# Converting three weight sets of the second layer beside the seven-product phase, and spacing the third chunk's attention at four steps a slot

## The chip, the cores and the metric

The kernel runs on one core of one Trainium2 chip. Each core has five engines with a queue of their own that run in order: TensorE (PE, whose weight loads are shown apart as PEld), VectorE (DVE), ScalarE (ACT), GpSimd (POOL) and SyncE (SP, which here issues nearly all DMAs). The metric is device microseconds of one execution; lower is better.

## The reference, cut to what matters

```python
x = attention(q, k, v)                 # 4 batches, 8 heads, 576 positions, banded masks; (2304, 512)
h = x @ w_in;  g = h * sigmoid(h)      # first layer, 512 -> 2048
x = g @ w_out                          # 2048 -> 512
a = x @ w1;  b = x @ w2                # second layer, 512 -> 1024 each
out = (a * b @ w3) @ w_out2            # 1024 -> 1024 -> 512
```

The weights come in a wide format of two 32-bit words a number. All products are made from pairs of reduced-precision numbers: each operand is split into a high part and a low part (the rest), and a product takes three matmuls, high by high, high by low and low by high. Converting a weight therefore means: load 512 KB of raw words; one ACT operation that rebiases the high words in place (`rebias`); two DVE operations that put the bits together (`bits`); an ACT copy that rounds to the high part (`high`) and a DVE subtraction that leaves the low part (`low`).

## The kernel before

The order of all work is written out by hand; the engines follow it in order and wait on each other by semaphores.

**First layer.** The 2304 tokens go in five chunks `CH1` of 512, 512, 256, 512 and 512. A chunk runs over 16 blocks `f` of the inner dimension; a *slot* is one block: the first product of the next block (`h_part`, two halves `h` and `H`), tanh and a multiplication (`t`), the split (`g`) and the second product of this block (`x2_part`, halves `x` and `X`). The strings in `SLOT` say in which order a slot's pieces are emitted. The letter `a` emits the next step of the attention of later chunks. `ATT` lists the eight steps by which two units of attention go through: V and S (values, and the scores of the next pair), M (maximum), E and O twice (exponential, output of the pair before), N (normalise: two small DVE operations and one POOL product a unit), L (loads), T (transposes), W (evacuation). The next pair's V waits for this pair's W, and the scores of the pair after it are emitted with that V. The letter `p` emits one operation from a list `todo`: first sums of weights and later 22 operations `late` that make sums of activations, and after the last slot whatever is left of it and four operations `last_`.

The third chunk (c = 2) has 256 tokens, so its 24 matmuls a slot are shorter. Its slots (`SLOT[1]`) hold five `a` and four `p`. Going through the lists by hand: the attention steps end with slot 7 of its 15, and `late` is emitted four a slot in slots 7 to 12.

**Seven-product phase.** The fourth chunk's first product is made for blocks p and p + 8 together by seven products of half size (`HPROD`, `h_product`, loop over p = 0 to 7). The products S1 to S4 take sums of weights that `sums_ops` left in DRAM (`swd`); `load_sw` brings those of the next p into four tiles `sw0` to `sw3` of a pool `sp`. A product goes to one of four banks; `collect_h` takes it out with DVE and ACT, and the product four places later writes that bank. Between the products stand the matmuls of the fourth chunk's second product (`x_some`, 24 a p), on `ga` of the p before.

**Late stage.** Sixteen blocks of the fifth chunk's second product, 12 matmuls each, and beside each block up to seven operations (`LATE_MICROS`) of the `Jobs` object `cv2`, which converts the second layer's weights: eight pieces of the output weights (WO), the sixteen pieces of w3, and eight *sets* a to h. A set holds a block of w1 or w2 for seven products: it is made from two raw pieces, with sums (`combine`), 7 units of 512 columns in all, and is also stored to DRAM (`setd`, by `set_io`) since it is used in three rounds. Its target is a pair of tiles `wf`. `free_at` says from which block on a job's target is free; `allowed` keeps `high` from running further. The order of the jobs is `0 1 a b 2 3 4 5 6 7 c 8 ...`. From the fifth block on one operation of a list `begin` is emitted too, on the activations that `load_x2` loads at the stage's start.

**Weights stage.** w3 times the output weights, in pieces k = 0 to 15 of 12 matmuls (`wp_group`, two parts of 6). k = 0 to 8 run back to back; the parts of k = 9 to 15 stand between the fourteen products of sets a and b. `weights(k, part)` first makes sure that piece k is converted, then emits four operations of `cv2` and the group, and after the first five groups one split of activations (`x_split`). w3 pieces alternate between two tiles, so piece k + 2 is rounded only when the matmuls of k are done. `x2_store(4, ...)` takes the fifth chunk out, its second half at k = 3 through a tile that has one buffer.

After that the sets run in three rounds of eight; in rounds two and three `set_io(s, False)` loads a set from DRAM.

Of the kernel before, what the change touches and what calls it, by code (L numbers as in the profile page):

```python
# [8 lines left out]
F32 = mybir.dt.float32  # L9
# [8 lines left out]
P = 128  # L18
# [52 lines left out]
ATT = "V2S0|M0|E1O3|E0O2|N0|L1|T0|W0"  # L71
SLOT = (
    ("ahapHppaxptapgX", "ahappHpxaptaXpg"),
    ("hHaatapagxapXpp", "hHaatapagxapXpp"),
)
LATE_MICROS = 7
GROUP = ("mmmmw", "mmmmW")
MICROS = ("2223332", "3332121")
LAST = "00 01 02 20 21 13 22 14 33 34 15 35".split()
# [9 lines left out]
def tile_kernel(  # L89
# [46 lines left out]
    def f32(ap):  # L136
        return ap.bitcast(F32)
# [526 lines left out]
    SET, W3, WO = {}, {}, {}  # L664
    for jt in range(NG):
        WO[jt] = cv2.add([wo2[jt]], lambda jt=jt: wo2_t(jt))
    for what in "0 1 a b 2 3 4 5 6 7 c 8 9 10 11 12 13 14 15 d e f g h".split():
        if what.isdigit():
            w3_add(int(what))
        else:  # L670
            set_add("abcdefgh".index(what))
    LATE = [8, 9, 10, 11, 6, 7, 0, 1, 2, 3, 4, 5, 12, 13, 14, 15]
    free_at = [jt // 2 for jt in range(NG)] + [4, 5, 7, 9]

    wp_ps = []

# [174 lines left out]
    sw = {}  # L851

    def load_sw(p, u):
        if p < NP:
            sw[u] = sp.tile([P, 512], F32R, tag=f"sw{u}", name=f"sw_{p}_{u}")
            nc.sync.dma_start(out=f32(sw[u]), in_=swd[p][:, u])

    def h_product(p, i, ps):
        w, x = HPROD[i]
        n = 0  # L860
        for kt in range(2):
            for sa, sb in ((0, 0), (1, 0), (0, 1)):
                if w[0] == "S":
                    lhs = sw[int(w[1]) - 1][:, 256 * sa + P * kt:256 * sa + P * kt + P]
                else:
                    lhs = block(p + NP * (int(w[0]) - 1), int(w[1]) - 1, sa)[:, P * kt:P * kt + P]
                rhs = t_block(int(x[1]), sb, kt) if x[0] == "T" else x_block(int(x[0]) - 1, int(x[1]) - 1, sb, kt)
                out_ = ps.rearrange("p (a n) -> p a n", a=2) if x == "T3" else ps
                nc.tensor.matmul(out_, lhs, rhs, start=(n == 0), stop=(n == 5))
                n += 1  # L870
        if w[0] == "S":
            load_sw(p + 1, int(w[1]) - 1)
# [4 lines left out]
    def x_mm(c, f, g, m, sa, sb, first_, last):  # L877
        nc.tensor.matmul(  # L878
            xps[c][m], wout(f, sa, m), g[:, sb],
            start=(first_ and sa == 0 and sb == 0), stop=(last and sb == 1),  # L880
        )

    PROD = [("11", "11"), ("S2", "T2"), ("12", "21"), ("S3", "T3"), ("S1", "T1"), ("22", "T4"), ("S4", "22")]
    B_AT = {name: i for i, (_, name) in enumerate(PROD)}
# [184 lines left out]
    with tc.manual_schedule():  # L1069
# [43 lines left out]
        x2_store(0, (0, 2))  # L1113

        slots = [(c, f) for c in range(3) for f in range(NF)]
        conv.close()
        todo = [op for p in range(NP) for op in sums_ops(p)]
        early, late, last_ = t_ops()
        todo += early
# [1 line left out]
        for i, (c, f) in list(enumerate(slots))[NF:-1]:  # L1121
            nxt = slots[i + 1]
            for x in SLOT[c - 1][att.half()]:
                if x == "h":
                    if nxt[1] == 0:
                        att.need(2)
                    h_part(*nxt, 0)
                elif x == "H":
                    h_part(*nxt, 1)
                    if nxt[1] == NF - 1:  # L1130
                        att.limit = (c + 3) * PER_B
                elif x == "t":
                    g_tanh(*nxt)
                    g_mul(*nxt)
                elif x == "g":
                    g_high(*nxt)
                    g_low(*nxt)
                elif x in "xX":
                    x2_part(c, f, "xX".index(x))
                    if x == "X" and f == NF - 1:  # L1140
                        x2_store(c, (0, 2))
                elif x == "a":
                    if not att.step() and c == 2 and "T" not in tmps:
                        attn.close()
                        parts_ = ctx.enter_context(ExitStack())
                        sp = parts_.enter_context(tc.tile_pool(name="sp", bufs=1, side="right", reuse_waits="tile"))
                        tmps["T"] = [sp.tile([P, 2, 2, 512], F32R, tag=f"T{n}", name=f"T{n}") for n in range(2)]
                        for u in (0, 1, 2, 3):
                            load_sw(0, u)
                        todo += late  # L1150
                elif x == "p" and todo and (len(todo) > len(early) or c == 2 and (att.out >= 3 * PER_B + 6 or "T" in tmps)):
                    todo.pop(0)()
        for op in todo + last_:
            op()

# [71 lines left out]
        def first_x(p):  # L1227
            return [(f, z) for f in (p, p + NP) for z in x_todo()]

        def x_some(c, todo, n, final):  # L1230
            for f, z in todo[:n]:
                x_mm(c, f, ga[f] if c == 3 else g_late(f), *z, first_=f == 0, last=f == final)
            del todo[:n]

        xs = []
        for p in range(NP):
            if p == 1:
                bank = [ps_x.tile([P, 512], F32, tag="x", name=f"hx{k}") for k in range(4)]
                xps[3] = [(ps_h if m < 2 else ps_a).tile([P, 512], F32, tag="h" if m < 2 else "a", name=f"x2_3_{m}")
                          for m in range(KT)]  # L1240
            for j, i in enumerate((0, 2, 4, 1, 3, 5, 6) if p == 0 else range(7)):
                live[i] = bank[done[0] % 4]
                done[0] += 1
                h_product(p, i, live[i])
                if p == 0 and j < 2:
                    x2_part(2, NF - 1, j)
                    if j == 1:
                        x2_store(2, (0, 2))
                        raws = [rawp.tile([P, 2, 512], F32, tag="raw", name=f"c_{k}") for k in range(3)]
                        cs.update({"s1": raws[0][:, 0], ("u2", 0): raws[0][:, 1], ("u2", 1): raws[1][:, 0],  # L1250
                                   "u3": raws[1][:, 1], "c22": raws[2][:, 0]})
                        ts += [raws[2][:, 1], gp.tile([P, 512], F32, tag="t", name="t_s", bufs=1)]
                        collect_h(0, 0)
                elif p == 0:
                    for k in {1: (1, 2), 3: (3, 4), 5: (5,), 6: (6,)}.get(i, ()):
                        collect_h(0, k)
                else:
                    collect_h(p, i)
                x_some(3, xs, 4 if i < 3 else 3, NF - 1)
            xs = first_x(p)  # L1260
        finish_h(NP - 1)
        x_some(3, xs, 24, NF - 1)
        x2_store(3, (0, 2))
        parts_.close()
        tmp1 = ctx.enter_context(tc.tile_pool(name="tmp1", bufs=1, side="right", reuse_waits="tile"))
        y2p = ctx.enter_context(tc.tile_pool(name="y2p", bufs=2, side="right", reuse_waits="tile"))
        x2p = ctx.enter_context(tc.tile_pool(name="x2p", bufs=1, side="right", reuse_waits="tile"))
        cv2.load()
        load_x2(0)
        begin = [lambda i=i: x_sum(i) for i in range(2)]  # L1270
        for i, name in ((2, "11"), (3, "T2")):
            begin += [lambda z=name: x_high(z), lambda z=name: x_low(z), lambda i=i: x_sum(i)]
# [1 line left out]
        for i, f in enumerate(LATE):  # L1274
            for z in x_todo():
                x_mm(4, f, g_late(f), *z, first_=i == 0, last=i == NF - 1)
            cv2.allowed = sum(z <= i for z in free_at)
            if i >= 4 and begin:
                begin.pop(0)()
            for _ in range(LATE_MICROS):  # L1280
                cv2.micro()
# [16 lines left out]
        def weights(k, part):  # L1298

            if (k, part) == (3, 0):  # L1300
                x2_store(NC1 - 1, (2,))
            if part == 0:
                cv2.allowed = W3[min(k + 1, 2 * NG - 1)] + 1
                cv2.need(W3[k])
                if k < NG:
                    cv2.need(WO[k], False)
            for x in GROUP[part]:
                if x == "m":
                    cv2.micro()
# [39 lines left out]
        for pr in range(NPR):  # L1349
            for k, s in enumerate(order(pr)):  # L1350
                if pr == 0 and k < 2:
                    continue
                if pr == 0:
                    cv2.allowed = min(len(cv2.jobs), SET[min(s + 3, NSET - 1)] + 1)
                    cv2.need(SET[s], False)
# [65 lines left out]
```

## Time and profile before

| | us |
|---|---|
| median of 3 runs | 822.84 (819.27 to 822.99) |
| profiled execution, its own time | 822.29 |
| its span, first to last instruction | 820.5 |
| PE busy in the span | 793.5 (97%) |
| DVE busy | 556.4 (68%) |
| ACT busy | 345.9 (42%) |

The busy time of PE includes matmuls that ran while the granted clock was low, so it is no measure of what could be saved. The times below are counted from the span's start. In a row of the timeline, the number in brackets is the idle time of the engine before that piece, and behind the arrow stands what ended it.

### The profile page before, as it was taken

How to read it: one execution, taken by the hardware profiler on the slowest of the kernel's cores; microseconds unless marked ns; L12 is line 12 of the kernel's file. 1: busy time of each engine (PE TensorE's matmuls, PEld its weight loads, DVE VectorE, ACT ScalarE, POOL GpSimd, SP SyncE). 2: the span in 40 equal slices, each digit the busy share in tenths (PEclk: the TensorE clock that was granted, in tenths of full speed). 3: DMA queues.
4: the chain of work that ended last, by engine and by line, in shares of the span. 5: the costliest groups of instructions: out<-in, count | busy, mean ns of one | idle time of the engine just before them, and what ended most of it. 6: DMA issues, size and time to landing. Idle time of an engine off the chain costs nothing. (4 is left out here: it accounts for less than half of the span.)

```text
span 820.5 us, 13242 instructions
## 1 busy us (share of the span) xinstructions
PE 793.5 (97%) x4829; PEld 684.5 (83%) x4829; DVE 556.4 (68%) x1321; ACT 345.9 (42%) x855; POOL 61.7 (8%) x90
## 2 busy tenths in 40 slices
PE   8999999999997899999999997899999999999997
PEld 7788888888887797888888875789999999999996
DVE  6989983766665375666565897668878654774544
ACT  7778863545354443334233564333423211221111
POOL 4101110101001100000000000002310000000000
PEclk9999999999998899999999999899999999999999
DMA  9788631533243202121116796625640751035202
GB/s 248 237 265 258 197 112 40 176 136 121 92 151 106 67 1 77 65 77 65 65 39 234 262 316 213 244 92 208 255 177 1 252 190 70 1 142 205 90 1 77
DMA packets 50513, 115.42 MB, mean 141 GB/s; under 512 B 4752, under 2 KB 22928, under 8 KB 48400
## 3 DMA queue, kind: packets, MB, share of 16 engines
q1 hardware_dynamic: 50160, 114.35, 41.6%
q8 instruction: 38, 0.62, 0.3%
q10 hardware_dynamic: 288, 0.23, 0.1%
q14 instruction: 27, 0.22, 0.1%
HBM read 82.05 MB, written 32.51 MB: 140 GB/s over the span
## 5 line engine op out<-in xcount | busy, mean ns | idle before, releaser
L977 PE MATMUL bank<-xT,wf 128*128 128x384 f32 x864 | 163.6, 335 | 0.0
L977 PEld LDWEIGHTS bank<-xT,wf 128*128 128x128 f32 x864 | 151.8, 188 | 6.4 <-DVE u L999 0.6
L749 PE MATMUL x<-g,wf 128*128 128x512 f32 (+1 forms) x576 | 124.1, 361 | 0.0
L709 PE MATMUL h<-xT,wf 128*128 128x512 f32 (+1 forms) x576 | 121.5, 359 | 0.0
L1033 PE MATMUL o<-wf,wf 128*128 128x512 f32 x429 | 110.0, 393 | 0.0
L749 PEld LDWEIGHTS x<-g,wf 128*128 128x128 f32 x576 | 96.4, 192 | 15.7 <-issue 0.2
L709 PEld LDWEIGHTS h<-xT,wf 128*128 128x128 f32 x576 | 96.5, 192 | 15.4
L1033 PEld LDWEIGHTS o<-wf,wf 128*128 128x128 f32 x429 | 79.5, 188 | 12.7
L688 PE MATMUL wp<-wf,wf 128*128 128x512 f32 x192 | 51.7, 417 | 10.4 <-ACT wf L600 9.0
L1013 ACT ACTIVATE wf<-c 128x384 fp32r<-128x384 f32 x48 | 25.2, 526 | 84.1 <-DVE c L1011 83.9
L995 ACT ACTIVATE s<-bank 128x384 f32<-128x384 f32 x24 | 11.8, 492 | 102.0 <-PE bank L977 91.4
L688 PEld LDWEIGHTS wp<-wf,wf 128*128 128x128 f32 x192 | 37.8, 201 | 20.4 <-ACT wf L600 10.3
L727 DVE SCALAR_TENSOR_TENSOR t<-t,h 128x512 f32<-128x512 f32 (+1 forms) x48 | 28.6, 596 | 36.4 <-ACT t L723 35.9
L878 PE MATMUL x<-ga,wf 128*128 128x512 f32 x192 | 51.9, 391 | 0.0
L278 POOL TENSOR_TENSOR sm<-sm,rs 128x288 f32<-128x288 f32 x36 | 31.7, 893 | 228.0 <-DVE su L271 133.1
L263 ACT ACTIVATE sm<-sm,nm 128x96 f32<-128x96 f32 x108 | 39.1, 365 | 23.1 <-DVE nm L253 23.0
L723 ACT ACTIVATE t<-h 128x512 f32<-128x512 f32 (+1 forms) x48 | 25.2, 526 | 51.8 <-PE h L709 48.5
L878 PE MATMUL x<-wf 128*128 128x512 f32 x192 | 43.7, 389 | 0.0
L878 PEld LDWEIGHTS x<-ga,wf 128*128 128x128 f32 x192 | 36.0, 188 | 8.0
L878 PEld LDWEIGHTS x<-wf 128*128 128x128 f32 x192 | 36.0, 188 | 7.5
L1002 DVE TENSOR_TENSOR c<-u,bank 128x384 f32<-128x384 f32 x36 | 19.9, 553 | 32.7 <-PE bank L977 32.6
L737 DVE TENSOR_TENSOR g<-t,g 128x512 fp32r<-128x512 f32 (+1 forms) x48 | 29.2, 609 | 16.7 <-ACT g L732 16.5
(158 smaller groups left out, 1216.0 us busy)
## 6 DMA issues: line engine op xcount, KB each, us to landing
rawj<-in_w_dram SPq DMA_DIRECT2D x32, 512.0 KB, 4.5
raw_i<-in_w_in_dram SPq DMA_DIRECT2D x16, 512.0 KB, 4.7
raw_u<-in_w_out_dram SPq DMA_DIRECT2D x16, 512.0 KB, 4.5
swd<-sw SPq DMA_DIRECT2D x16, 512.0 KB, 2.6
sw<-swd SPq DMA_DIRECT2D x32, 256.0 KB, 2.5
setd<-wf SPq DMA_DIRECT2D x8, 1024.0 KB, 3.9
wf<-setd SPq DMA_DIRECT2D x8, 1024.0 KB, 5.3
setd<-wf SPq DMA_DIRECT2D x8, 768.0 KB, 6.4
```

Of the source, the lines that this page charges most:

```text
L263: nc.scalar.activation(sm[:, j], sm[:, j], AF.Exp, bias=nm[:, j:j + 1], scale=-1.0, accum_out=su[:, j:j + 1],)
L278: nc.gpsimd.tensor_tensor(sm, sm, rs[:, :NB].to_broadcast([P, NB, KB]), op=ALU.mult)
L688: nc.tensor.matmul(wp_ps[i], a[:, i // 2, sa, i % 2 * P:(i % 2 + 1) * P], o[:, sb], start=(jt == 0 and x == 0), stop=(jt == NG - 1 and x = ...
L709: nc.tensor.matmul(ps, win(f, sa, kt), xT[:, kt, sb, r0:r0 + n], start=(kt == 0 and x == 0), stop=(kt == KT - 1 and x == 2),)
L723: nc.scalar.activation(gt[c, f], hps[c, f][:, :n], AF.Tanh, scale=0.5)
L727: nc.vector.scalar_tensor_tensor(t, t, 1.0, ps, op0=ALU.add, op1=ALU.mult)
L737: nc.vector.tensor_sub(g[:, 1], t, f32(g[:, 0]))
L749: nc.tensor.matmul(xps[c][m][:, :n], wout(f, sa, m), g[:, sb], start=(f == 0 and sa == 0 and sb == 0), stop=(f == NF - 1 and sb == 1),)
L878: nc.tensor.matmul(xps[c][m], wout(f, sa, m), g[:, sb], start=(first_ and sa == 0 and sb == 0), stop=(last and sb == 1),)
L977: nc.tensor.matmul(b, a_op(s, a, sa, kt), b_op(x, sb, kt), start=(n == 0), stop=(n == 5),)
L1013: behind.append((count[0] + 1, lambda: nc.scalar.activation(hi, c[k], AF.Copy)))
L1033: nc.tensor.matmul(ps, g_block(jj, n, sa)[:, m % 3 * P:(m % 3 + 1) * P], wp_v(f, sb)[:, c0:c1], start=((first_ or len(parts) == 2) and x = ...
```

## The change

The sets a, b and c leave `cv2`. Their conversion is written out as 78 operations (`set_ops`, 26 a set) that are emitted one or two behind each product of the seven-product phase, from the fourth product of p = 0 on: by the counts written into the loop they end behind the third product of p = 7. One raw tile `w` serves all of them: first as the landing place of a raw piece, then as two buffers for units that go to `setd`. In the weights stage the three sets are loaded back from `setd` at k = 1, 3 and 6 (`SET_AT`).

To make room, the S1 sums of weights have no tile of their own: `load_sw` puts them where block 21 of the first layer's weights stood, which no product reads, and the load for p = 0 stands behind the third chunk. The pool that holds `y` closes after the phase. `load_x2(0)` moves to block 6 of the late stage and `begin` starts at block 8. The third chunk's slots get four `a` and three `p`, with the steps in other places.

```diff
 SLOT = (
     ("ahapHppaxptapgX", "ahappHpxaptaXpg"),
-    ("hHaatapagxapXpp", "hHaatapagxapXpp"),
+    ("ahaHtapxgpaXp", "ahHapxtgpXaap"),
 )
+SET_AT = (1, 3, 6)
...
-    for what in "0 1 a b 2 3 4 5 6 7 c 8 9 10 11 12 13 14 15 d e f g h".split():
+    for what in "0 1 2 3 4 5 6 7 8 9 10 11 12 13 14 15 d e f g h".split():
...
-    free_at = [jt // 2 for jt in range(NG)] + [4, 5, 7, 9]
+    free_at = [jt // 2 for jt in range(NG)] + [4, 5]
...
     def load_sw(p, u):
-        if p < NP:
+        if p < NP and u == 0:
+            dst = f32(wf[p + NP])[:, :1024].rearrange("p (s n) -> p s n", s=2)[:, :, :256]
+            nc.sync.dma_start(out=dst, in_=swd[p][:, 0].rearrange("p (s k) -> p s k", s=2))
+        elif p < NP:
             sw[u] = sp.tile([P, 512], F32R, tag=f"sw{u}", name=f"sw_{p}_{u}")
...
+                if w == "S1":
+                    lhs = block(p + NP, 0, sa)[:, P * kt:P * kt + P]
...
+    def set_ops(s, t, w):
...
+        def high(k, x):
+            nc.scalar.activation(o[:, k, 0].bitcast(F32R), x, AF.Copy)
+
+        def low(k, x, at):
+            nc.vector.tensor_sub(o[:, k, 1].bitcast(F32R), x, o[:, k, 0])
+            if at is not None:
+                nc.sync.dma_start(out=setd[s][:, at], in_=o[:, k].rearrange("p s k -> p (s k)"))
+
+        q = []
+        for i in range(2):
+            q += [lambda i=i: load(i), lambda i=i: rebias(i), lambda i=i: bits(i, 0), lambda i=i: bits(i, 1)]
+        for k, u in enumerate((0, 1, 3, 2)):
+            q += [lambda u=u: total(u), lambda k=k: high(k % 2, t), lambda k=k, u=u: low(k % 2, t, u)]
+        for k, (i, h) in enumerate(((0, 0), (0, 1), (1, 1))):
+            q += [lambda k=k, i=i, h=h: high(k % 2, half(i, h)),
+                  lambda k=k, i=i, h=h: low(k % 2, half(i, h), 4 + k)]
+        return q
...
-        conv.close()
...
-                        for u in (0, 1, 2, 3):
+                        for u in (1, 2, 3):
...
+        load_sw(0, 0)
         for op in todo + last_:
             op()
...
+                        w = rawp.tile([P, 512, 2], I32, tag="raw", name="set_raw")
+                        t = sp.tile([P, 256], F32, tag="set_t", name="set_t")
+                        sets = [op for s in range(SETS) for op in set_ops(s, t, w)]
...
                 x_some(3, xs, 4 if i < 3 else 3, NF - 1)
+                for _ in range(2 if i in (1, 2, 3, 5) else 1):
+                    if sets and (p or j > 2):
+                        sets.pop(0)()
...
         cv2.load()
-        load_x2(0)
...
-            if i >= 4 and begin:
+            if i == 6:
+                load_x2(0)
+            if i >= 8 and begin:
                 begin.pop(0)()
...
+                if k in SET_AT:
+                    set_io(SET_AT.index(k), False)
```

The functions inside `set_ops` that are left out above do the same as those of `Jobs`: `load` a 512 KB DMA into `w`, `rebias` one ACT operation, `bits` two DVE operations of 512 columns, `total` one DVE sum of 256 columns.

## Rows read from the trace of the kernel before

**Rows 1.** Busy time by stretch: third chunk, first p, phase, late stage, weights stage.
```profile
core 0: us, PE busy (x) PEld busy (x) DVE busy (x) ACT busy (x) POOL busy (x), PEclk, DMA share, GB/s
243.11:312.17 69.06, 61.88 (x601) 57.87 (x600) 37.54 (x129) 30.50 (x106) 6.15 (x8) 0.93 0.18 61
312.17:324.99 12.82, 11.65 (x57) 9.16 (x55) 7.90 (x14) 4.11 (x9) 0.00 (x0) 1.00 0.34 104
324.99:436.92 111.93, 111.93 (x487) 91.19 (x486) 71.83 (x113) 40.66 (x69) 0.00 (x0) 1.00 0.18 59
436.92:480.44 43.52, 43.52 (x193) 36.04 (x192) 31.94 (x57) 20.72 (x35) 0.00 (x0) 1.00 0.81 290
480.44:520.66 40.22, 29.82 (x110) 22.25 (x108) 32.74 (x55) 21.01 (x35) 0.00 (x0) 0.87 0.79 273
```

**Rows 2.** Waits within the third chunk: total us, times, longest.
```profile
PE t L289 <- POOL sm L278: 6.9, 5, 2.1
```

**Rows 3.** Timeline of PE in the third chunk: start, us, what.
```profile
278.18 1.21 PE L233 MATMUL o<-qk 64*64 64x96 f32 x24
...
285.36 1.16 PE L289 MATMUL t<-ident,sm 128*96 128x128 f32 x6 [0.74 <-POOL sm L278]
...
289.13 1.60 PE L709 MATMUL h<-xT,wf 128*128 128x256 f32 x12
290.57 1.60 PE L749 MATMUL x<-g,wf 128*128 128x256 f32 x12
```

**Rows 4.** Timeline of ACT and POOL beside the same pair of units.
```profile
281.84 0.39 ACT L723 ACTIVATE t<-h 128x256 f32<-128x256 f32 x1 [1.08 <-PE h L709]
...
284.36 1.57 POOL L278 TENSOR_TENSOR sm<-sm,rs 128x288 f32<-128x288 f32 x2 [9.40 <-DVE su L271]
```

**Rows 5.** Timeline of PE in the weights stage.
```profile
480.44 5.60 PE L688 MATMUL wp<-wf,wf 128*128 128x512 f32 x24
...
488.76 6.89 PE L688 MATMUL wp<-wf,wf 128*128 128x512 f32 x22 [0.47 <-DVE wf L604]
497.44 11.45 PE L688 MATMUL wp<-wf,wf 128*128 128x512 f32 x48 [1.79 <-ACT wf L600]
514.60 1.22 PE L688 MATMUL wp<-wf,wf 128*128 128x512 f32 x2 [5.71 <-ACT wf L600]
```

**Rows 6.** Timeline of ACT in the weights stage.
```profile
496.27 0.60 ACT L763 ACTIVATE x2s<-x 128x512 f32<-128x512 f32 x1 [3.73 <-DMA x2d<-x2s]
...
508.42 1.06 ACT L600 ACTIVATE wf<-ss 128x1024 fp32r<-128x1024 f32 x1 [1.17 <-DVE ss L582]
```

**Rows 7.** Timeline in the seven-product phase: one product in two successive p, and an evacuation.
```profile
342.48 1.55 PE L869 MATMUL hx<-T,sw 128*128 128x512 f32 x6
...
351.35 0.68 DVE L1204 TENSOR_TENSOR c<-c,hx 128x512 f32<-128x512 f32 x1
...
357.69 1.55 PE L869 MATMUL hx<-T,sw 128*128 128x512 f32 x6
```

**Rows 8.** Groups by line and shape: busy us, mean ns, idle before and its releasers.
```profile
L263 ACT ACTIVATE sm<-sm,nm 128x96 f32<-128x96 f32 x108 | 39.1, 365 | 23.1 <-DVE nm L253 23.0
L561 DVE SCALAR_TENSOR_TENSOR y<-rawj,y 128x512 int32<-128x512 int32 x40 | 27.7, 692 | 1.2
L551 ACT ACTIVATE rawj<-rawj 128x512 f32<-128x512 f32 x40 | 26.3, 671 | 21.2 <-DMA rawj<-in_wo_dram 11.0 <-DMA rawj<-in_w_dram 10.1
L556 DVE TENSOR_SCALAR y<-rawj 128x512 int32<-128x512 int32 x40 | 17.0, 426 | 10.8 <-ACT rawj L551 9.8
L604 DVE TENSOR_TENSOR wf<-y,wf 128x256 fp32r<-128x256 f32 x8 | 3.4, 419 | 0.0
L600 ACT ACTIVATE wf<-y 128x256 fp32r<-128x256 f32 x8 | 3.3, 409 | 1.7 <-DVE y L561 1.7
```

**Rows 9.** Tile views: DMA line of the raw tiles, then of the sums of weights.
```profile
DMA to landing us min/median/max: 3.1/5.3/8.0
...
DMA to landing us min/median/max: 2.5/2.6/5.0
```

More of the change, by code (lines that the diff above doesn't have):

```diff
@@ L862, in h_product @@
             for sa, sb in ((0, 0), (1, 0), (0, 1)):
-                if w[0] == "S":
+                if w == "S1":
+                    lhs = block(p + NP, 0, sa)[:, P * kt:P * kt + P]
+                elif w[0] == "S":
                     lhs = sw[int(w[1]) - 1][:, 256 * sa + P * kt:256 * sa + P * kt + P]
@@ L881, in x_mm, with load, rebias, bits @@
         )
+    SETS = 3
+    def set_ops(s, t, w):
+        src = (w1, w2)[s % 2]
+        raw, o = w, f32(w.rearrange("p n w -> p (n w)")).rearrange("p (u s k) -> p u s k", u=2, s=2)
+        y = {}
+        def load(i):
+            nc.sync.dma_start(out=raw.rearrange("p n w -> p (n w)"), in_=src[s // 2 + i * NG // 2].bitcast(I32))
+        def rebias(i):
+            h = raw[:, :, 1].bitcast(F32)
+            nc.scalar.activation(h, h, AF.Prelu, scale=2.0 ** -112, alpha=2.0 ** 32)
+        def bits(i, x):
+            if x == 0:
+                y[i] = yp.tile([P, 512], I32, tag="y", name=f"ys_{s}_{i}")
+                nc.vector.tensor_single_scalar(y[i], raw[:, :, 1], 3, op=ALU.logical_shift_left)
+            else:
+                nc.vector.scalar_tensor_tensor(
+                    y[i], raw[:, :, 0], 29, y[i], op0=ALU.logical_shift_right, op1=ALU.bitwise_or
+                )
+        def half(i, k):
+            return f32(y[i])[:, 256 * k:256 * k + 256]
+        def total(u):
+            if u == 0:
+                nc.vector.tensor_add(t, half(1, 0), half(1, 1))
+            elif u == 1:
+                nc.vector.tensor_sub(t, t, half(0, 0))
+            elif u == 3:
+                nc.vector.tensor_sub(t, half(0, 1), t)
+            else:
+                nc.vector.tensor_sub(t, half(0, 0), half(1, 0))
+        def high(k, x):
[13 more added lines that the diff above has]
+        return q
     PROD = [("11", "11"), ("S2", "T2"), ("12", "21"), ("S3", "T3"), ("S1", "T1"), ("22", "T4"), ("S4", "22")]
@@ L1233, in x_some @@
             del todo[:n]
-        xs = []
+        xs, sets = [], []
         for p in range(NP):
@@ L1259, in tile_kernel @@
                 x_some(3, xs, 4 if i < 3 else 3, NF - 1)
+                for _ in range(2 if i in (1, 2, 3, 5) else 1):
+                    if sets and (p or j > 2):
+                        sets.pop(0)()
             xs = first_x(p)
         finish_h(NP - 1)
+        assert not sets
         x_some(3, xs, 24, NF - 1)
@@ L1264, in tile_kernel @@
         parts_.close()
+        conv.close()
         tmp1 = ctx.enter_context(tc.tile_pool(name="tmp1", bufs=1, side="right", reuse_waits="tile"))
@@ L1354, in tile_kernel @@
                     cv2.allowed = min(len(cv2.jobs), SET[min(s + 3, NSET - 1)] + 1)
-                    cv2.need(SET[s], False)
+                    if s in SET:
+                        cv2.need(SET[s], False)
                 if k == NSET - 4 and pr + 1 < NPR:
```

## The prediction

> **What bounds the kernel now.** I read the busy time by stretch first [rows 1]. The reader is to see where PE is not full: in the phase and in the late stage it is busy in all 111.93 and all 43.52 us at full clock, so nothing is to be won there, only lost. It is not full in the third chunk (69.06 us, granted clock 0.93) and in the weights stage (40.22 us, 0.87). DVE is busy in 71.83 of the phase's 111.93 us, but in 32.74 of the weights stage's 40.22. Then I read who waits for whom in these two stretches, then their timelines.
>
> Third chunk: PE waited 6.9 us in five waits, all for POOL's product ahead of the transposes [rows 2], and a mean clock of 0.93 over 69.06 us loses another 0.07 x 69.06 = 4.8. So 11.7 us lie there beside what the matmuls themselves take.
>
> Weights stage: k = 0 and 1 took 5.60 us for 24 matmuls [rows 5], 0.233 each; 108 of them up to the end of k = 8 need 25.2. The stretch took 40.22 [rows 1], so 15.0 are lost: a clock of 0.87 is 5.2 of that, the rest is waits for the conversion. The longest (5.71) stands before k = 8 [rows 5]; the ACT timeline shows in front of it the rounding of a set's sums, which is set c's (508.42) [rows 6]. The one of 1.79 ends when the fifth chunk's second half has been copied out, and that copy stood 3.73 us for a DMA store [rows 6]. Behind the wait of 0.47, 22 matmuls took 6.89 instead of 5.1 (low clock: +1.8), while behind the one of 1.79 the 48 took 11.45, 0.239 each (full clock) [rows 5].
>
> **Part 1: conversions out of the late and weights stages.** A set costs DVE four `bits` operations, 2 x (0.43 + 0.69), and eleven of 256 columns at 0.42: 6.9 us; ACT two `rebias` at 0.67 and seven roundings at 0.41: 4.2 us [rows 8]. Without c the weights stage's DVE work falls from 32.74 to 25.9, against PE's 25.2; what the late stage left over of set b goes too, and I don't size it. So DVE can just keep pace. What is late next is the alternation of two tiles: piece k + 2 is rounded (0.60, as the copy of as many columns [rows 6]) and its rest taken (0.69 as L561 [rows 8]) while k + 1 runs (12 x 0.233 = 2.8 us), which leaves about 1.2 us with the steps between them, and five activation splits stand between in the first three k. I take 1.5 us as lost there. Gain: 15.0 - 1.5 = **13.5**. Bounds: 15.0, and 7.5 if only c's wait goes (5.71 and one spell of low clock, 1.8).
>
> The loads from `setd` that come instead are 128 x 7 x 512 x 4 bytes, 1.75 MB, each: 5.25 MB where before the stores of b and c (3.5) and c's raw pieces (1.0) stood, little more for the DMA engines. Their targets are free since the late stage, so SP doesn't stand on them, and their first use is after k = 8, over 20 us later. Of what SP has behind them (raw pieces of w3) four lie in SBUF ahead. `load_x2` at block 6 and `begin` from block 8 move within a stage in which PE waits for neither (43.52 of 43.52 busy [rows 1]); `begin` still ends with block 15. All of these at nothing; if a raw piece came late, a wait like that of 1.79, held in the lower bound.
>
> **Part 2: the third chunk at four steps a slot.** A slot is 24 matmuls, 2 x (290.57 - 289.13) = 2.88 us [rows 3]. Two slots now hold exactly one pair of units. Between the end of a pair's scores and its transposes PE will have 48 matmuls, 5.76 us. The chain beside it: before, in the pair of 278.18, tanh started at 281.84 and POOL at 284.36, 2.52 later, with the exponentials of one unit between, and the transposes 1.0 after POOL [rows 3, 4]. Now tanh comes ahead of both units: it waits for the first two half slots (1.6 us), and one more unit is 3 x 0.365 and an output, 0.41 at most as a copy of 256 columns [rows 8], 1.5. So the transposes can start 1.6 + 2.52 + 1.5 + 1.0 = 6.6 us after the scores: PE waits 0.9 for them and 0.3 for the second POOL product, 1.2 a pair, 4.8 for four. A wait of 1.2 should not cost clock, as that of 1.79 did not. Gain: 11.7 - 4.8 = **6.9**. Bounds: 0 (waits and clock as before) and 11.7. I take the value worked out from the nearest pair.
>
> The sums of activations run three a slot and end late: four of `late` are left behind the last slot, 4 x 0.69 = 2.8 us of DVE before the first sums. That stretch has DVE busy in 7.90 of 12.82 us [rows 1] and its first sum waits for the fourth product: nothing. Without that cover it would be 2.8.
>
> **Part 3: 78 operations in the phase.** Three sets bring DVE 3 x 6.9 = 20.6 us and ACT 12.6. DVE has 111.93 - 71.83 = 40.1 us free, 5.4 in each p of 357.69 - 342.48 = 15.21 us [rows 1, 7]. The work fits; the waits are the question. `load` and `rebias` are emitted back to back, so ACT stands until the piece has landed (3.1 us at least [rows 9]) and behind it stand the copies, tanhs and roundings of `collect_h`, for which DVE waits. The second and third set's first load also waits until the previous set's last store has landed (2.5 [rows 9]), since both use `w`.
>
> The third set as an example, from the end of the last `low` at (p = 5, product 0): store landed 3.0, load landed 6.5, `rebias` done 7.2, both `bits` done 8.3, the sum of product 3 done 9.0 where the timeline of before has it at 4.6: 4.4 late. The second load goes out after these `bits`; its `rebias` ends 4.4 after them, and the sum of product 5 is 5.1 late. The same count gives 5.5 for the second set and 4.9 for the first.
>
> The reserve is the four banks: the sum ends at 352.03 (351.35 + 0.68), the product that reuses its bank starts at 357.69 [rows 7]: 5.7 us. So one set alone is hidden; what PE pays is lag carried over. A p gives DVE 5.4 free less 2.8 of new work, and in a lagging p some of the rest goes to waits for ACT. I count 2.4 us still carried when the second set begins and 3.7 at the third: 2.4 + 5.5 - 5.7 = 2.2 and 3.7 + 5.1 - 5.7 = 3.1; the first set falls into the first p, where sums are packed close, and I put 0.7 there. Loss: **6.0**. Bounds: 0 and 4.9 + 5.5 + 5.1 = 15.5, with no reserve at all.
>
> The rule that speaks against this part stands in the Trainium skill, "DMA: Bandwidth & Descriptors", section Rules for kernel authors: issue a DMA early, compute, and wait on its semaphore late. Here each load is waited for at once. The trace agrees: ACT's `rebias` of before stood 21.2 us for loads [rows 8], in a stage where PE did not depend on it. By the rule alone all six waits would show, which is the third rival.
>
> The S1 sums go to another place by as many DMAs of the same size (2.5 us to land [rows 9]), one p ahead; the one for p = 0 has the first two products and two half slots to land. SP passes 21 stores and 6 loads more; a store waits at SP for DVE, and behind it stand the next p's sums, needed 15 us later. Nothing for both; without that cover one landing, 2.5.
>
> **Sum.** 822.3 (the profiled execution's own time) - 13.5 - 6.9 + 6.0 = 807.9, so **808**. That execution lies 0.5 below the median of the runs, which I leave aside.
>
> **Rivals.**
> 1. The phase hides everything: DVE's 40.1 free us against 20.6 and short lags. For it: PE is never late in the phase now. Against it: the lags above nearly fill the reserve one by one. 808 - 6 = 802. Chance 0.22.
> 2. The third chunk gives nothing: V waits for W, so the pair's chain sets the pace whatever PE does beside it. For it: all five waits have one releaser. Against it: the wait was only 0.74 where 42 matmuls stood in the chain. 808 + 6.9 = 815. Chance 0.12.
> 3. All six landings reach PE: 15.5 instead of 6. Against it: the banks' 5.7 us. 817.5. Chance 0.12.
> 4. The weights stage keeps all but c's wait: 808 + 6 = 814. Chance 0.08.
> 5. Slower than before: in the phase DVE never catches up, because each lagging p also waits for ACT's roundings, and PE pays the lags and the new work, 15.5 + 20.6 = 36: 838. It decides from a loss above 13.5 + 6.9 = 20.4 on. Against it: 40.1 free us. Chance 0.06.
>
> **How the numbers follow.** My forecast has 0.40. The measurement tells about 0.5%, 4 us, from no change, so faster means below 818.7: the forecast, rivals 1, 2 and 4 (0.82) and half of rival 3, whose 817.5 lies at that bound: 0.88; its other half, 0.06, is the same; rival 5, 0.06, is slower. The range goes from rival 1 with the full 15.0 in the weights stage and 2 more in the third chunk (798) to rival 3 (818).
>
> **What would show it.** In the phase, ACT's `rebias` of the new raw tile waits for its DMA six times, 2 to 5 us each, and PE's matmuls of `h_product` show waits for DVE or ACT of about 6 us in all, most at p = 3 and 5. The weights stage is about 27 us long at full clock, with no wait above 1.8. In the third chunk POOL still ends PE's waits, four of about 1 us, the clock stays at 1.00 and the stretch takes some 62 us. The forecast is wrong if the phase grows by more than 12 us or not at all, if a clock below 0.95 stays in either stretch, or if a wait for a DMA appears in the weights stage.

## The result, and the profile after

The changed kernel took 813.54 us (median of 4 runs, 812.69 to 814.56) against 821.66 (4 runs, 819.27 to 822.99) of the kernel before: a ratio of 0.9905, interval 0.9875 to 0.9934. The forecast was 808, range 798 to 818. The profiled execution took 812.69, so 9.6 less than the 822.29 of before.

The same five stretches as in [rows 1], from the windows view of the changed kernel (same columns):

```profile
243.44:305.62 62.18, 58.05 (x602) 54.07 (x602) 34.82 (x125) 28.84 (x104) 5.69 (x8) 1.00 0.21 67
305.62:318.46 12.84, 11.69 (x57) 9.17 (x55) 8.77 (x16) 4.10 (x9) 0.00 (x0) 1.00 0.47 144
318.46:441.57 123.11, 116.85 (x487) 92.77 (x486) 89.11 (x160) 51.76 (x99) 0.00 (x0) 0.97 0.37 120
441.57:485.12 43.55, 43.55 (x193) 36.04 (x192) 26.41 (x43) 17.38 (x28) 0.00 (x0) 1.00 0.73 253
485.12:510.82 25.70, 25.21 (x109) 19.93 (x107) 19.82 (x33) 15.78 (x28) 0.00 (x0) 1.00 0.92 347
```

Against [rows 1]: third chunk -6.88 (forecast -6.9), weights stage -14.52 (forecast -13.5), phase +11.18 (forecast +6.0); the first p and the late stage stand still. Two terms came out near the forecast; the phase lost almost twice what was put down for it. These three make 10.2 us; the 0.6 that is missing to 9.6 went before the third chunk and behind the weights stage.

The waits of the phase in the changed kernel (total us, times, longest): those for the loads into the new raw tile, DVE's behind them, and all of PE's matmuls:

```profile
ACT set_raw L902 <- DMA set_raw<-in_w_dram: 23.1, 6, 8.1
DVE ys L907 <- ACT set_raw L902: 14.1, 5, 6.4
...
PE hx L875 <- DVE c L1259: 3.4, 2, 2.4
...
PE x L884 <- ACT ga L1229: 1.9, 1, 1.9
...
PE hx L875 <- DVE c L1254: 0.5, 1, 0.5
PE x L884 <- DVE c L1274: 0.5, 1, 0.5
```

The chain reads from the top down: ACT's `rebias` (L902) stands six times for its load, DVE's `bits` (L907) stands behind it, and the products (L875) stand for the evacuations (L1254, L1259) that are queued on DVE behind the `bits`. The waits of PE sum to 6.3, but the phase grew by 11.2. Where the rest is, the timeline of PE tells: the product that opens each p (p = 1 opens at 318.46, p = 7 at 416.90), and the end of the phase.

```profile
318.46 1.52 PE L875 MATMUL hx<-xT,wf 128*128 128x512 f32 x6
...
334.58 1.54 PE L875 MATMUL hx<-xT,wf 128*128 128x512 f32 x6
...
349.78 1.54 PE L875 MATMUL hx<-xT,wf 128*128 128x512 f32 x6
...
366.98 1.66 PE L875 MATMUL hx<-xT,wf 128*128 128x512 f32 x6 [0.97 <-DVE c L1259]
...
382.30 1.54 PE L875 MATMUL hx<-xT,wf 128*128 128x512 f32 x6
...
400.06 2.93 PE L875 MATMUL hx<-xT,wf 128*128 128x512 f32 x6 [2.40 <-DVE c L1259]
404.00 1.55 PE L875 MATMUL hx<-T,sw 128*128 128x512 f32 x6
...
416.90 1.54 PE L875 MATMUL hx<-xT,wf 128*128 128x512 f32 x6
...
431.41 3.77 PE L884 MATMUL x<-ga,wf 128*128 128x512 f32 x15
437.12 4.61 PE L884 MATMUL x<-ga,wf 128*128 128x512 f32 x12 [1.94 <-ACT ga L1229]
```

A p without a wait takes 15.20 us (334.58 to 349.78). By this measure, in which a wait in front of the product that opens a p counts to the p before, p = 1 lost 0.9, p = 3 2.0, p = 5 2.6, p = 4 0.1. Then p = 6 lost 1.6 without any wait of its own: its first six matmuls took 2.93 instead of 1.54, and the second product came 3.94 after the first instead of 2.3. From 437.12 the last twelve matmuls took 4.61; and the stretch from 416.90 to the phase's end at 441.57 is 24.67, 4.0 more than the 20.66 of the kernel below in which nothing waits. 0.9 + 2.0 + 0.1 + 2.6 + 1.6 + 4.0 = 11.2.

The set of p = 5 and 6 in detail, from the timeline of SP, ACT and DVE:

```profile
392.60 0.33 SPq L898 DMA_DIRECT2D set_raw<-in_w_dram  x1
...
397.57 0.65 ACT L902 ACTIVATE set_raw<-set_raw 128x512 f32<-128x512 f32 x1 [8.14 <-DMA set_raw<-in_w_dram]
398.26 0.43 DVE L907 TENSOR_SCALAR ys<-set_raw 128x512 int32<-128x512 int32 x1 [6.38 <-ACT set_raw L902]
...
399.33 0.68 DVE L1259 TENSOR_TENSOR c<-c,hx 128x512 f32<-128x512 f32 x1
```

Load issued, 4.97 us to `rebias`, both `bits`, and only then the evacuation for which the product at 400.06 waits. The set before it issued its loads at 353.02 and 360.98 and went on 3.46 and 3.49 us later.

### The profile page after: what moved, and what is told of

The parts are those of the page before. It is cut to its first block, busy times and chain, and to the rows that moved or that the text cites. A ratio compares the mean times of both kernels' runs of the same rounds, so it can differ in the third digit from the quotient of the medians.

```text
span 810.9 us, 13315 instructions
## 1 busy us (share of the span) xinstructions
PE 791.5 (98%) x4829; PEld 681.0 (84%) x4829; DVE 555.8 (69%) x1333; ACT 345.9 (43%) x867; POOL 61.2 (8%) x90
## 5 line engine op out<-in xcount | busy, mean ns | idle before, releaser
L750 PE MATMUL x<-g,wf 128*128 128x512 f32 (+1 forms) x576 | 121.8, 357 | 0.0
L884 PE MATMUL x<-ga,wf 128*128 128x512 f32 x192 | 54.8, 406 | 2.4 <-ACT ga L1229 1.9
L1056 ACT ACTIVATE s<-bank 128x384 f32<-128x384 f32 x24 | 11.8, 491 | 103.3 <-PE bank L1038 92.7
L689 PE MATMUL wp<-wf,wf 128*128 128x512 f32 x192 | 46.9, 392 | 0.1
L689 PEld LDWEIGHTS wp<-wf,wf 128*128 128x128 f32 x192 | 35.7, 188 | 7.4 <-ACT wf L601 0.5
```

Source lines behind the costliest of these rows:

```text
L689: nc.tensor.matmul(wp_ps[i], a[:, i // 2, sa, i % 2 * P:(i % 2 + 1) * P], o[:, sb], start=(jt == 0 and x == 0), stop=(jt == NG - 1 and x = ...
L750: nc.tensor.matmul(xps[c][m][:, :n], wout(f, sa, m), g[:, sb], start=(f == 0 and sa == 0 and sb == 0), stop=(f == NF - 1 and sb == 1),)
L884: nc.tensor.matmul(xps[c][m], wout(f, sa, m), g[:, sb], start=(first_ and sa == 0 and sb == 0), stop=(last and sb == 1),)
```

## The experiments

One table for all; a stage is read from the windows of the profiled execution, whose own time stands in the last column. Apart from the first four and the kernel with three places of distance, each was run once, and the kernel before took 819.09 to 823.20 us beside them: their whole times are not compared here, their stages are. How well a phase repeats show the second and the fourth row, whose phases have the same code: 123.11 and 122.63.

| kernel | phase | weights stage | profiled execution |
|---|---|---|---|
| before | 111.93 | 40.22 | 822.29 |
| after | 123.11 | 25.70 | 812.69 |
| slots only | 111.93 | 41.70 | 818.52 |
| sets only | 122.63 | 25.36 | 821.34 |
| sets without their loads | 111.84 | 26.26 | 804.91 |
| three places of distance behind each load | 111.84 | 25.59 | 802.78 |
| two operations behind every product | 123.63 | 27.06 | 814.98 |
| the same, distance at first loads | 115.55 | 25.43 | 808.37 |
| the same, distance at second loads | 117.22 | 27.10 | 811.10 |
| the same, one place at each load | 118.34 | 26.32 | 809.26 |
| last five operations moved | 118.22 | 27.05 | 807.99 |
| two sets, three places of distance | 111.88 | 36.42 | 816.18 |

**The two halves apart: slots only.** The kernel before with the new `SLOT` row.

```diff
-    ("hHaatapagxapXpp", "hHaatapagxapXpp"),
+    ("ahaHtapxgpaXp", "ahHapxtgpXaap"),
```

> The kernel before with the third chunk's slots of the change and nothing else. My sum: the third chunk takes some 62 us instead of 69.06, every other stretch as before (phase 111.9, weights stage 40.2), the execution 6 to 7 us shorter, some 815. The rival, that the attention's chain sets the pace whatever stands beside it: less than 2 us shorter.

818.98 us (10 runs), ratio 0.9968, interval 0.9952 to 0.9983. From the first 256-column matmul to the first product of p = 0 it took 68.44 us, before 74.02, after 67.24; the phase did not move. The expected 6 to 7 us were missed: the medians differ by 3.3. In the profiled execution 1.2 us of the third chunk stand behind its wait of 1.69, where the clock fell, which it did not in the changed kernel, and 1.5 us went in the weights stage, which nothing of this edit touches.

**Sets only.** The changed kernel with the old `SLOT` row.

> The changed kernel with the third chunk's slots of before. If the parts add up: third chunk 69, weights stage 25.7 instead of 40.2 (-14.5), phase 123 instead of 111.9 (+11.2), so 3 us faster than before, some 819. If the parts depend on each other (the phase starting with DVE still busy from the new slots), the phase is under 121 here.

816.89 us (10 runs), ratio 0.9939, interval 0.9919 to 0.996; phase 122.63, weights stage 25.36, and the third chunk as before (74.08 in the measure used above). The profiled execution, 821.34, is the slowest of the ten. The medians fell by 3.3 and 5.4, together 8.7, against 8.1 for the whole change: the halves add up, to within what the medians can tell.

**Sets without their loads.** All operations stay; the six loads are left out and the tile holds a constant, so that the three sets are converted from other numbers.

```diff
-            q += [lambda i=i: load(i), lambda i=i: rebias(i), lambda i=i: bits(i, 0), lambda i=i: bits(i, 1)]
+            q += [lambda: None, lambda i=i: rebias(i), lambda i=i: bits(i, 0), lambda i=i: bits(i, 1)]
...
+                        nc.vector.memset(w.rearrange("p n w -> p (n w)").bitcast(F32), 1.0)
```

> The changed kernel without the six loads of raw pieces in the phase (the tile is filled once with a constant, so the three sets are made of wrong numbers); all other operations stay, with their stores. Theory of the landings: ACT no longer stands for DMAs, the phase falls from 123.1 to 112 to 115 us and the execution to some 803. Rival, the added work of DVE and ACT and the waits of a low part for its rounding: the phase stays above 119.

The windows view of the phase, and its waits on the new tile:

```profile
321.45:433.29 111.84, 111.84 (x488) 91.18 (x486) 88.00 (x158) 50.22 (x95) 0.00 (x0) 1.00 0.33 109
```

```profile
DVE set_raw L930 <- ACT set_raw L927: 8.3, 7, 1.6
ACT set_raw L902 <- DMA setd<-set_raw: 3.7, 2, 3.2
```

PE is full at full clock with 88.00 us of DVE beside it, nearly as many as in the changed kernel (89.11). So neither the new work nor the wait of `low` for `high` (8.3 us; 8.8 in the changed kernel) nor the wait for the last store of a set (3.2 at the longest) costs PE anything. All 11.2 us hang on the landings.

**Three places of distance.** Three empty places stand between each load and its `rebias`, and two operations behind every product, so that the longer list still ends in p = 7.

```diff
-            q += [lambda i=i: load(i), lambda i=i: rebias(i), lambda i=i: bits(i, 0), lambda i=i: bits(i, 1)]
+            q += [lambda i=i: load(i)] + 3 * [lambda: None] + [lambda i=i: rebias(i), lambda i=i: bits(i, 0), lambda i=i: bits(i, 1)]
...
-                for _ in range(2 if i in (1, 2, 3, 5) else 1):
+                for _ in range(2):
```

> Two operations behind every product, and three empty places between each load and its rebias, so that a load has about two products to land; the list still ends at p = 7. Theory of the landings: ACT's 23 us of waits for the raw tile fall below 10, the phase takes 115 to 118, the execution some 806. Rival, the work: the operations are packed closer where there are any, the phase stays at 121 to 125 us.

804.42 us (4 runs, 802.78 to 807.18), ratio 0.9805, interval 0.9773 to 0.9837: better than both kernels. Its windows of the phase and the weights stage, its waits for the load, and PE at the phase's end:

```profile
320.01:431.85 111.84, 111.84 (x488) 91.19 (x486) 87.85 (x158) 50.78 (x96) 0.00 (x0) 1.00 0.40 132
...
475.37:500.96 25.59, 25.17 (x109) 19.93 (x107) 19.80 (x33) 15.81 (x28) 0.00 (x0) 1.00 0.92 347
```

```profile
ACT set_raw L902 <- DMA set_raw<-in_w_dram: 4.2, 3, 2.0
```

```profile
411.19 1.54 PE L875 MATMUL hx<-xT,wf 128*128 128x512 f32 x6
...
425.70 6.31 PE L884 MATMUL x<-ga,wf 128*128 128x512 f32 x27
```

Six waits of 23.1 us have become three of 4.2, and the phase is as short as without any loads, shorter than the 115 to 118 that the theory gave. The 27 matmuls at the end run through.

**Two operations behind every product, no distance.** The second edit above alone.

> The changed kernel with two of the 78 operations behind every product (it has two behind four of the seven and one behind the others), so that they end early in p = 6 and not behind the third product of p = 7; each load is still waited for at once. Theory (landings, and at the end of the phase a reserve of its own that is much smaller than the banks' 5.7 us): the six waits of rebias stay, the PE waits inside the phase stay (p = 3 and p = 5, about 6 to 7 us with the clock they cost), and the loss in front of the last 12 matmuls of the phase (1.94 us of wait and a low clock, about 3.9 us) is gone: phase about 119 us, between 118 and 121. Rival (the loss at the end is late work that is carried over and has nothing to do with where the list ends): the phase stays at 123. Rival (packing the operations closer costs more in the middle than it saves at the end): 124 or more.

Phase 123.63: the theory's 118 to 121 is missed, and what happened is what the second rival says, just under its 124. The wait at the end is gone, but the middle of the phase lost 11.8 instead of 7.3; the waits there were 0.44, 3.42 and 3.03. It is also the base for the next three: against it, distance is worth 11.8 us, and closer packing alone gains nothing.

**Distance at the first or at the second loads only.** In place of `3 * [lambda: None]`: `3 * (i == 0) * [lambda: None]`, and `3 * (i == 1) * [lambda: None]`.

> Two operations behind every product, and three empty places between a set's first load and its rebias; the second load of each set is still waited for at once. The first load is the one that also waits for the previous set's last store. Theory (PE pays only when the lag of a first landing and that of the second add up beyond the banks' 5.7 us): three waits of rebias for a load stay, each 3.5 to 5 us, and nearly no loss is left: phase 112 to 114 us. Rival (each landing that is waited for costs PE its share): half of the loss of the kernel without empty places stays, 115 to 117.

> Two operations behind every product, and three empty places between a set's second load and its rebias; the first load, which waits for the store of the set before and then for its own landing, is still waited for at once. Theory (the lags add up): three waits of 6 to 8 us stay at the first rebias of a set (3.5 to 5 in the first set), and since 8 less the reserve of 5.7 already reaches PE, some of the loss stays: phase 113 to 116 us, in any case more than with the empty places at the first load. Rival (the second landing is the one that costs): as good as with empty places at both, 111.8.

Phases 115.55 and 117.22: 8.1 and 6.4 us better than 123.63, and both together 11.8. The first is outside the theory's range and inside the rival's, the second just outside the theory's. That the first load costs more than the second holds in these two executions, but hardly by PE's waits, 2.7 us in the first and 3.0 in the second: most of the 1.7 us between them are slower matmuls, above all those at the low clock behind the wait of 3.00. Nor did `rebias` stand as expected: four waits of 11.0 in all in the first, three of 13.0 in the second, the longest 5.0 and not 6 to 8. How a single landing gets to PE shows the timeline of the second kernel, set b's first load:

```profile
345.98 1.55 PE L875 MATMUL hx<-T,wf 128*128 128x512 f32 x6
...
348.06 1.52 PE L875 MATMUL hx<-xT,wf 128*128 128x512 f32 x6
...
351.98 0.68 DVE L1264 TENSOR_TENSOR c<-c,hx 128x512 f32<-128x512 f32 x1
...
354.78 0.33 SPq L898 DMA_DIRECT2D set_raw<-in_w_dram  x1
...
358.89 0.43 DVE L907 TENSOR_SCALAR ys<-set_raw 128x512 int32<-128x512 int32 x1 [5.03 <-ACT set_raw L902]
359.23 0.68 DVE L1269 TENSOR_TENSOR c<-c,hx 128x512 f32<-128x512 f32 x1
...
359.97 2.43 PE L875 MATMUL hx<-xT,wf 128*128 128x512 f32 x6 [3.00 <-DVE c L1269]
```

DVE was 4.4 late before the landing: at 351.98 it took out a product that had ended at 347.53. It then stood 5.03 for the landing, and the next product, ended at 349.58, was taken out at 359.23, 9.6 late. The banks hold 5.7 for the product of [rows 7] and 6.5 for this one (in the kernel before, it is out at 353.50 and its bank is written again from 360.00): 9.6 - 6.5 = 3.1, the wait of 3.00. The other two first landings of this kernel cost PE 0.4 us (p = 1) and 0.1 (p = 5). So one landing is hidden only where little lag is carried to it.

**One place at each load.** `1 * [lambda: None]`.

> Two operations behind every product and one empty place between each load and its rebias (three gave a phase of 111.84 us, none 123.63). Two places are one product and its matmuls of the second product, about 2.2 us. Theory (a load that lands after 3.6 to 5 us is hidden only by distance): ACT's waits for the load shrink by about 2 us each, from 21.0 to about 10 in six, and the phase lies between the two, 114 to 118 us. Rival (any distance frees the queue, since what cost was the order of the queue and not the landing): 112. Rival (the landing moves with it, because the DMA queue is what is slow): 122 or more.

The waits for the load fell from 21.0 to 11.6 us in six, as expected; the phase took 118.34, just above the theory's range and far from both rivals. The first place took 5.3 us off the phase, the next two 6.5.

**The last five operations moved.** The changed kernel, with nothing of the list behind the products of p = 7.

```diff
-                    if sets and (p or j > 2):
+                    if sets and (p or j > 2) and p < NP - 1:
...
         finish_h(NP - 1)
-        assert not sets
+        for op in sets:
+            op()
```

> The changed kernel with its own placing; only the last five of the 78 operations (two roundings on ACT, three subtractions on DVE with their stores), which stood behind the first products of p = 7, are emitted behind the last evacuation. Theory (the loss in front of the last 12 matmuls of the phase is the lag that p = 7 has no more room to work off, since nothing follows its last product but its own 24 matmuls): DVE is 2 us earlier at the end, the wait of 1.94 us falls under 1 us or goes, and the phase is 119 to 121 us instead of 123.11; the waits in p = 1, 3 and 5 stay. Rival (the lag is that of set c's landings in p = 5 and is carried to the end whatever stands in p = 7): the phase stays at 122.5 to 123.5.

Phase 118.22, a little under the theory's 119 to 121. The waits of p = 3 and 5 stay (0.30, 1.12 and 2.10), and the end runs through:

```profile
429.48 6.31 PE L884 MATMUL x<-ga,wf 128*128 128x512 f32 x27
```

So 4.0 us of the loss belong to p = 7 and are given back by five operations of at most 0.43 us on DVE and 0.42 on ACT. It takes both, these operations and a lag from the landings: without the loads the same five cost nothing. The late stage, where they went, stayed at 43.52.

**Two sets instead of three.** As with three places of distance, but set c is converted between pieces 7 and 8 of the weights stage, as in the kernel before.

```diff
-SET_AT = (1, 3, 6)
+SET_AT = (1, 3)
...
+    for what in "0 1 2 3 4 5 6 7 c 8 9 10 11 12 13 14 15 d e f g h".split():
...
-    SETS = 3
+    SETS = 2
```

> Only sets a and b in the phase, with two operations behind every product and three empty places behind each load; set c is converted where it was before, between pieces 7 and 8 of the weights stage. Tells how much of the gain in the weights stage is set c's alone. My prediction's step (set c alone: its wait of 5.71 us and one spell of low clock, 1.8 us): weights stage 25.6 + 7.5 = 33 us, phase 111.84. Rival (DVE keeps pace with c as soon as a and b are out of the late stage): weights stage 26 to 28 us. Rival (c is the whole of it, a and b brought nothing): near the 40.22 us of before.

Weights stage 36.42, 3.4 above the theory, far from the first rival and 3.8 below the second's 40.22. Its timeline of PE:

```profile
477.56 21.92 PE L689 MATMUL wp<-wf,wf 128*128 128x512 f32 x96
507.41 1.22 PE L689 MATMUL wp<-wf,wf 128*128 128x512 f32 x2 [7.93 <-ACT wf L601]
509.55 4.63 PE L689 MATMUL wp<-wf,wf 128*128 128x512 f32 x10 [0.92 <-DVE wf L605]
```

Eight pieces run through; the whole loss stands before k = 8, as waits of 7.93 and 0.92 and matmuls at half speed behind them (4.63 for ten). The timeline of ACT shows, ahead of the rounding of set c's sums, a raw piece of w3 that came late:

```profile
499.88 0.65 ACT L552 ACTIVATE rawj<-rawj 128x512 f32<-128x512 f32 x1 [5.35 <-DMA rawj<-in_w_dram]
...
501.26 1.04 ACT L601 ACTIVATE wf<-ss 128x1024 fp32r<-128x1024 f32 x1
```

Taking set c out of this stage is worth 36.42 - 25.59 = 10.8 us, sets a and b 40.22 - 36.42 = 3.8; how the 10.8 divide between c's operations and the late piece these runs don't tell.

## Why the prediction was right or wrong

The profiled execution took 4.8 us more than the sum of 807.9: part 1 gave 1.0 more than forecast, part 2 what was forecast, part 3 cost 5.2 more, and 0.6 went elsewhere.

**Part 1, the weights stage, was right, with its residue too high for this execution.** Forecast 13.5, measured 14.5; 108 matmuls ran through in one row.

```profile
485.12 25.27 PE L689 MATMUL wp<-wf,wf 128*128 128x512 f32 x108
```

The 1.5 us that I left there come and go: 25.4 to 25.7 us in four kernels with this conversion, 26.3 in two and 27.1 in three. In the kernel with the five operations moved, where it is 27.05, PE waited once, before the last piece, and ACT shows for what:

```profile
ACT rawj L552 <- DMA rawj<-in_w_dram: 5.1, 1, 5.1
...
PE wp L689 <- ACT wf L601: 1.4, 1, 1.4
```

A raw piece of w3 came late. In the changed kernel the same wait of ACT was 3.8 us and did not reach PE. Over the nine kernels with this conversion, PE waited for nothing where ACT's wait for that piece was 3.4 to 3.8 us, 0.6 and 0.7 where it was 4.4, and 1.4 to 1.5 where it was 5.1 to 5.2; ACT's waits for the alternating tiles were 4.2 us in three in all nine. So the limit is not the alternation of two tiles that I took for it, but the landing that I had held in the lower bound. Why it lands sooner or later was not tried. DVE had more room than the "just keep pace" that I gave it: it was busy in 19.82 us of the stage, not 25.9, because what the late stage had left over of sets a and b, which I did not size, was another 5.1 (32.74 before, 27.64 with c alone). The bound for "only c's wait goes", 7.5, was too low: c, with the late piece, brought 10.8.

**Part 2, the third chunk, was right in its mechanism; that it met its number is in part luck.** The rows that answer to [rows 2, 3], waits of the stretch and then from the timeline of PE one pair, the transposes of the next and the scores behind them:

```profile
PE t L290 <- POOL sm L279: 3.5, 4, 1.7
```

```profile
245.43 1.70 PE L710 MATMUL h<-xT,wf 128*128 128x256 f32 x12
...
251.99 1.16 PE L290 MATMUL t<-ident,sm 128*96 128x128 f32 x6 [0.55 <-POOL sm L279]
...
263.05 1.16 PE L290 MATMUL t<-ident,sm 128*96 128x128 f32 x6 [1.68 <-POOL sm L279]
...
265.29 1.21 PE L234 MATMUL o<-qk 64*64 64x96 f32 x24
```

The 48 matmuls from 245.43 on fill the chain up to the transposes, and POOL still ends the four waits. The chain was forecast at 6.6 us from the end of the scores to the transposes; its four instances took, from the first matmul behind the scores, 6.56, 7.69, 6.78 and 6.57. The waits were 0.55, 1.68, 0.76 and 0.55, 3.5 in all, where I had 0.9 each and 0.3 for a second product of POOL that these rows don't show apart. So the waits gave 3.3 us instead of 2.1, and the rest of the stretch 3.5 instead of the 4.8 that I had put down for the clock: two misses that cancel. And I said of four equal waits, "A wait of 1.2 should not cost clock"; one of them came out at 1.68, and that it cost none is luck of this execution. All ten kernels with the new slots wait 1.68 or 1.69 at this place; the third chunk, in the measure of the experiments, took 67.24 to 67.27 in three of them, 68.44 to 68.62 in four and 69.78 to 69.82 in three, against 74.02 before. The kernel with distance at the second loads is one of the last three; its 24 score matmuls behind the wait took 2.19 us where the changed kernel's took 1.21:

```profile
263.44 1.15 PE L290 MATMUL t<-ident,sm 128*96 128x128 f32 x6 [1.69 <-POOL sm L279]
...
266.01 2.19 PE L234 MATMUL o<-qk 64*64 64x96 f32 x24
```

The granted clock over the 4 us from the end of this wait was 1.00 in the first three and 0.57 to 0.70 in the other seven. So the gain is 4.2 to 6.8 us by this measure, as the clock falls or not. Why it falls in one execution and not in the next these runs don't tell.

**Part 3, the phase, failed at one term: "The reserve is the four banks", 5.7 us, for all of the phase.** My sum was 0.7 + 2.2 + 3.1 = 6.0 for the three sets. Measured were 0.9, 2.1 (p = 3 and 4) and, up to the end of the wait, 2.6, together 5.6 (4.3 of them waits, the rest slower matmuls): the size of the three terms held. How much lag is still carried, 2.4 and 3.7, the sum took without working it out, so part of that agreement may be chance. What the sum did not have are two things, 5.6 us between them:

- At the end of the phase there are no banks to spare. Behind the last product stand only matmuls that need `ga` of this same p, so a small lag reaches PE at once: 4.0 us, of which 1.94 are the wait and most of the rest a low clock (4.61 for twelve matmuls). Moving five operations took all of it away. My sentence "what PE pays is lag carried over" looked at the products and forgot the last 24 matmuls.
- The wait of 2.40 in p = 5 was followed by a low clock, 1.6 us. I had counted clock for the weights stage and none for the phase.

The landing was sized well enough: from issue to `rebias` four of the six took 3.39 to 3.65 us (I had 3.5), two 4.97 and 5.45. Of the signs of being wrong that I named, one came: a wait for a DMA in the weights stage, ACT's 3.8 us. It did not reach PE.

**The rivals.** The first (all of it hidden, 802) is not what this kernel does, but what three places of distance make of it: 804.42. The third (all six landings reach PE) falls in its size, since 11.2 is less than 15.5; that the landings are the cause it shares with my sum. The rule named there, from the Trainium skill's page "DMA: Bandwidth & Descriptors", section Rules for kernel authors, that a DMA is issued early and waited for late, is borne out by the runs. With 0, 1 and 3 places between issue and wait the phase took 123.63, 118.34 and 111.84 us. (Of the 21.2 us that I gave for ACT's `rebias` before, 14.2 stand in the late stage, where PE was full; 3.3 stand in the weights stage, where it was not.) The second and the fourth fall with the third chunk's and the weights stage's windows. The fifth, that DVE never catches up, falls too: with 88.00 us of work on DVE and no landing, PE lost nothing.

Left open: why two operations behind every product make the middle of the phase 4.5 us worse than the changed kernel's own spacing. Of the 4.5, 2.6 are longer waits, and the rest is mostly slower matmuls behind them. The longest wait, 3.42, is that of a matmul of the second product for `ga`, not for a bank, so the banks are not the only reserve in the middle either. That the denser list leaves less time to work off a lag fits the rows, and was not tried by itself.

## What to carry to other kernels

When conversion work is put beside a stage that fills the main engine, count the work against the free time of the engine that does it, but count the waits by queue: an operation that waits for a load holds everything behind it on its engine, so emit the load some operations ahead of its first reader (here three places, at two behind each product of 2.2 us, were worth 11.8 us). Take the reserve of each place by itself: inside a rotation of buffers it is the rotation's, at the end of the stage it is only what follows the last producer. And test a lag with the landing taken out and the work left in: that tells in one execution whether the work or the wait is the price.

## What the runs showed of the hardware that was not expected

PE's clock after a wait. Mean granted clock by the windows view, the changed kernel in three stretches, the first and the last of them beginning where the waits of 2.40 and of 1.94 end:

```profile
400.00:404.00 4.00, 3.94 (x11) 3.13 (x11) 2.58 (x6) 1.50 (x3) 0.00 (x0) 0.58 0.80 261
404.00:408.00 4.00, 4.00 (x19) 3.28 (x18) 3.96 (x8) 1.66 (x4) 0.00 (x0) 1.00 0.00 2
437.00:441.57 4.57, 4.45 (x12) 3.51 (x13) 2.25 (x4) 1.74 (x5) 0.00 (x0) 0.63 0.00 0
```

0.58 and 0.63 are mostly the lower of its two levels (0.50, 1.2 GHz); from 404.00 on it is at the full 2.4 GHz again. It was the same behind the wait of 3.00 in the kernel with distance at the second loads (0.58 over 4.0 us). Waits of 0.97 and of 1.54 were followed by products of 1.66 us, nearly full speed, and in the kernel before one of 1.79 by 48 matmuls at full speed [rows 5]. The low clock that [rows 5] shows behind a wait of 0.47 stands behind two waits, because another had ended shortly before:

```profile
487.55 0.73 PE L688 MATMUL wp<-wf,wf 128*128 128x512 f32 x2 [1.51 <-ACT wf L600]
```

The wait of 1.68 or 1.69 in the third chunk, with the same work around it, was followed by a granted clock of 1.00 over 4 us in three kernels' executions and of 0.57 to 0.70 in seven. So the length of the last wait alone does not decide. The waits of 2.40 and of 3.00 cost 1.6 and 1.9 us of clock on top (the p in which the second stands took 20.05 us instead of 15.20), which belongs into the sum of any stage that fills PE, as a range that begins at nothing.
